# End units' transposes moved behind the next scores in two batches, low parts ahead of gathers, in a block-sparse attention kernel with a gated projection

## The chip, the cores and the metric

The kernel runs on one core of a Trainium2 chip. The metric is device time in microseconds (us) of one execution, the median over several runs. TensorE is PE in the profile (PEld is its weight load), VectorE is DVE, ScalarE is ACT, GpSimd is POOL, and SyncE, which issues most DMAs, is SP.

## The reference

Four batches, eight heads, 768 positions, head size 64. Attention is block sparse in blocks of 32: a block of queries sees its neighbours, the first and last block, and three drawn blocks. The first and last block of queries see everything. The result goes through a causal five-tap gate and two products with 512 x 512 weights.

```python
scores = scale * np.matmul(q, k.transpose(0, 1, 3, 2))
mask = np.abs(blk_i - blk_j) <= window
mask = mask | (blk_i == 0) | (blk_j == 0) | (blk_i == n_blocks - 1) | (blk_j == n_blocks - 1)
# and for every query block its three sampled key blocks
attn = np.exp(scores - max) / sum
x = np.matmul(attn, v)
gate_pre[s] = sum_k conv_w[k] * x[s - 4 + k]
out = (sigmoid(gate_pre) * (x @ w_val)) @ w_out
```

Everything is float32. The projections keep that precision by splitting each operand into a high part in a rounded format and a low part, and adding three products.

## The kernel before

The work is cut into 52 **units**, 13 a batch. Eleven units of a batch are pairs of inner query blocks. Two are **end units**, which hold the first and the last query block, see all 768 keys, and stand behind four to six pairs (`GLOB_AT`). Loop step n issues the scores of unit n, its softmax, the values of unit n-2, and the transposes of unit n-1, with pieces of the projection (`fill`, counted by the table `FILLS`) and of its preparation (`prepare`, counted by `STEPS`) between. A helper chains each engine's instructions in the order in which the Python code issues them, so each engine works through one list in order.

One unit: TensorE makes scores (tile `sc`, for an end unit four tiles `s`) in PSUM. VectorE takes the maxima (`mx`). ScalarE makes the exponentials (`pe`, for an end unit `first`, `rest`, `first`, `rest`). TensorE transposes them (`pt`, two buffers), ScalarE evicts them (`ptr`, three buffers), and TensorE multiplies with the values (`av`). VectorE divides (`rs`, `x`), TensorE transposes the result (`xp`), and ScalarE writes it to `xT`. An end unit has three groups of transposes and three evictions, a pair two. The PSUM tag `sc` has three buffers, which the scores and `xp` share.

The values of a pair's own and sampled blocks come in `vb` (three buffers) by two gathers, indirect DMAs that POOL issues (`load_values`). A gather for the unit three pairs on waits until `av` has read the buffer.

The projection of 384 rows (`project`, two a batch, eight in all, here called P1 to P8) has four groups `vp`, one for each of 128 channels f, and three row groups `op`. When group f is done, `evict(f)` makes `y` on VectorE (two buffers) and the high part `yh` on ScalarE. `second(f)` makes the low part `yl` on POOL. In the kernel before, `second(3)` is issued only after the first half of the first `op`, and the first `op` has the products with `yl` in its second half. `split` makes high and low parts `xh`, `xl` of the next rows in the same way; POOL has the `xl`. The gate's multiply-adds (`th`, 128 in all) are VectorE's. The two weight matrices arrive as words that VectorE decodes during batches 0 and 1 (`words`, with a cast on ScalarE).

`before_last_low` holds the gathers of a step back once only, in the step whose first half reaches the group behind the last `vp`. The functions `block_rows` and the branch on `SP_VALUES` are never entered, as the four tuples of `SP_VALUES` are empty; the tile `sv` is allocated all the same.

Of the kernel before, what the change touches and what calls it, by code (L numbers as in the profile page):

```python
# [19 lines left out]
NP = NB // 2  # L20
DM = H * D
DV = D + 1
CH = 4
# [20 lines left out]
SP_VALUES = ((), (), (), ())  # L44
REGS = 4
# [19 lines left out]
def attention_moe(ctx, tc, qb, kb, v, ve, sampled, w_val, conv_w, w_out, ident_in, slot_in, out):  # L65
# [33 lines left out]
    sb = const.tile([128, NB, NR, 2], I32, name="sb")  # L99
# [10 lines left out]
    ones = const.tile([128, 256], F32, name="ones")  # L110
# [9 lines left out]
    sf = const.tile([128, NR, NB], F32, name="sf")  # L120
# [11 lines left out]
    vm = const.tile([128, NR, NB], F32, name="vm")  # L132
    tmp = const.tile([128, NR, NB], F32, name="tmp")
# [19 lines left out]
    sv = const.tile([1, B, 2, NP - 1, NR], I32, name="sv")  # L153
    sk = tmp[0:1]

    def block_rows(b):

        dve.tensor_scalar_add(sk, sf[0:1], float((b - B) * NB))
        dve.tensor_tensor(out=sk, in0=sk, in1=vm[0:1], op=ALU.mult)
        for j in SP_VALUES[b]:  # L160
            dve.tensor_scalar_add(sv[:, b, j].rearrange("p i r -> p r i"), sk[:, :, 1 + j : NB - 1 : 2], float(B * NB))

# [10 lines left out]
    wv = [const.tile([128, CH, DM], F32R, name=f"wv{n}") for n in range(2)]  # L173
# [143 lines left out]
    def load_values(pr):  # L317
# [5 lines left out]
        if pr.p == 0 and SP_VALUES[b]:  # L323
            block_rows(b)
# [7 lines left out]
        for j, i in enumerate(PAIRS[pr.p]):  # L332
            if j in SP_VALUES[b]:
                near = i + (1 if j else -1)
                near = (b * NB + near if 0 < near < NB - 1 else B * NB) * BLK
                sp.dma_start(pr.vb[0:BLK, j, :], v[near : near + BLK, :])
                if pr.p % REGS == 0:
                    held[j] = nc.values_load_multi_w_load_instructions(
                        sv[0:1, b, j, pr.p : min(pr.p + REGS, NP - 1), :].rearrange("p i r -> p (i r)"), engines=[SP],
                        min_val=0, max_val=B * NB,  # L340
                        skip_runtime_bounds_check_because="block numbers are drawn from [0, 24)",
                    )[1]
                for r, reg in enumerate(held[j][pr.p % REGS * NR : pr.p % REGS * NR + NR]):
                    sp.dma_start(
                        pr.vb[BLK * (r + 1) : BLK * (r + 2), j, :],
                        v.rearrange("(n k) d -> n k d", k=BLK)[bass.ds(reg, 1)].rearrange("o k d -> (o k) d"),
                    )
                continue
            pool.indirect_dma_start(
                out=pr.vb[:, j, :], out_offset=None, in_=v,  # L350
                in_offset=bass.IndirectOffsetOnAxis(ap=idx[:, b, i : i + 1], axis=0),
            )
# [21 lines left out]
    def scores(un):  # L374
        pr = un.pr
        un.P = []
        if pr.glob:
# [10 lines left out]
            mx = three.tile([128, 2, 4], F32, tag="mx", name="mx")  # L388
            rest = five.tile([128, 2, 256], F32, tag="pr", name="rest")
            for h in range(2):  # L390
                dve.tensor_reduce(out=mx[:, h, 0:1], in_=lo[h], axis=AX.X, op=ALU.max, negate=True)
                dve.tensor_reduce(out=mx[:, h, 1:2], in_=hi[h][:, 0:256], axis=AX.X, op=ALU.max, negate=True)
                dve.tensor_tensor(out=mx[:, h, 2:3], in0=mx[:, h, 0:1], in1=mx[:, h, 1:2], op=ALU.min)
                first = five.tile([128, 512], F32, tag="pr", name="first")
                act.activation(rest[:, h, :], hi[h][:, 0:256], AF.Exp, bias=mx[:, h, 2:3])
                act.activation(first, lo[h], AF.Exp, bias=mx[:, h, 2:3])
                un.P.append(first)
            un.P.append(rest.rearrange("p h k -> p (h k)"))
            return
        sc = [ps_sc.tile([128, 2, 256], F32, tag="sc", name="sc") for _ in range(2)]  # L400
        kt = pr.kg.rearrange("p (t e) x -> p t e x", e=4)
        for a in range(2):
            for t in range(2) if a and pr.bt.b >= SPLIT else (slice(0, 2),):
                for g in range(4):
                    for h in range(2):
# [8 lines left out]
                        )  # L414
        mx = three.tile([128, 2, 4], F32, tag="mx", name="mx")
# [7 lines left out]
    def transposes(un):  # L423
        un.PT = []
        for p in un.P:
            pt = ps_pt.tile([128, 4, 128], F32, tag="pt", name="pt")
            for c in range(4):
                transpose(pt[:, c, :], p[:, 128 * c : 128 * c + 128], ident)
            t = three.tile([128, 4, 128], F32, tag="ptr", name="ptr")
            act.copy(t, pt)  # L430
            un.PT += [t[:, c, :] for c in range(4)]
            yield
# [118 lines left out]
    def project(m):  # L551
# [35 lines left out]
        evict(CH - 1)  # L587
        gating.discard(id(m))
# [14 lines left out]
        for r in range(m.n // 128):  # L603
# [3 lines left out]
            for f, yn, w in terms + [(CH - 1, yh, wo[0]), (CH - 1, yh, wo[1]), (CH - 1, yl, wo[0])]:  # L607
                matmul(op, yn[:, f, r * 128 : (r + 1) * 128], w[:, f, :], start=n == 0, stop=n == 11)
                n += 1
                if n == 6:  # L610
# [3 lines left out]
                    if r == 0:  # L614
                        second(CH - 1)
# [46 lines left out]
    def before_last_low(times):  # L662

        return may_project() and to_project[0][0].groups <= CH + 1 < to_project[0][0].groups + times
# [39 lines left out]
    for n in range(N + LAG_V):  # L704
# [25 lines left out]

        if n < N:
            scores(units[n])
        if n == 0:
# [12 lines left out]
        if n >= LAG_V and not before_last_low(int(FILLS[min(2 * n, len(FILLS) - 1)])):  # L746
            next_values()
        if 0 <= n - LAG_T < N:
            for half, _ in enumerate(transposes(units[n - LAG_T])):
# [3 lines left out]
                if n >= LAG_V:  # L753
# [68 lines left out]
```

## Time and profile before

| | us |
|---|---|
| median of three runs | 384.92 (383.56 to 385.92) |
| the profiled execution, time / span | 385.59 / 383.8 |
| busy: PE / PEld / DVE / ACT / POOL | 350.1 / 275.0 / 264.1 / 253.6 / 221.0 |

A row of the timeline has the start and the length of a run of like instructions, the engine, the operation with output and inputs, the count, and in brackets how long the engine stood idle before and what ended that. A row of the windows has the busy time of each engine in a stretch, with counts, then the granted TensorE clock (1.00 is 2.4 GHz), the DMA share and GB/s. TensorE's trace has two records for each matmul of the program. "issue" is time for which the profile shows no cause.

### The profile page before, as it was taken

How to read it: one execution, taken by the hardware profiler on the slowest of the kernel's cores; microseconds unless marked ns; L12 is line 12 of the kernel's file. 1: busy time of each engine (PE TensorE's matmuls, PEld its weight loads, DVE VectorE, ACT ScalarE, POOL GpSimd, SP SyncE). 2: the span in 40 equal slices, each digit the busy share in tenths (PEclk: the TensorE clock that was granted, in tenths of full speed). 3: DMA queues.
4: the chain of work that ended last, by engine and by line, in shares of the span. 5: the costliest groups of instructions: out<-in, count | busy, mean ns of one | idle time of the engine just before them, and what ended most of it. 6: DMA issues, size and time to landing. Idle time of an engine off the chain costs nothing.

```text
span 383.8 us, 15523 instructions
## 1 busy us (share of the span) xinstructions
PE 350.1 (91%) x6274; PEld 275.0 (72%) x6274; DVE 264.1 (69%) x546; ACT 253.6 (66%) x619; POOL 221.0 (58%) x309
## 2 busy tenths in 40 slices
PE   8788869878967999999899979999999999999895
PEld 7365556556646887788679857787787879789794
DVE  4346476866897779477978877656769877959520
ACT  1857697887788758765776756756666766565321
POOL 1885566897486486757553266556633753444640
PEclk9969999999999999999999989999999999999999
DMA  7997982999991546789786337788773373110102
GB/s 235 300 300 238 344 278 59 280 263 300 320 297 52 133 126 195 217 286 286 205 241 213 81 108 226 203 271 246 205 203 112 96 224 113 33 56 30 56 28 84
DMA packets 52584, 72.37 MB, mean 189 GB/s; under 512 B 6944, under 2 KB 34720, under 8 KB 52512
## 3 DMA queue, kind: packets, MB, share of 16 engines
q1 hardware_dynamic: 44896, 47.69, 40.7%
q0 software_dynamic: 7040, 23.43, 21.1%
q8 instruction: 50, 0.82, 0.9%
q10 hardware_dynamic: 576, 0.24, 0.2%
q14 instruction: 22, 0.18, 0.2%
HBM read 65.05 MB, written 6.29 MB: 186 GB/s over the span
## 4 chain that ended last, share of the span: by engine, by line
PE 65%; DVE 16%; ACT 7%; issue 6%; POOL 3%; DMA 1%; ACTq 1%; DVEq 0%
PE av L83 13%; PE op L83 13%; PE vp L83 13%; PE sc L83 11%; PE pt L83 9%; DVE th L83 7%; DVE mx L83 4%; PE xp L83 3%; PE s L83 3%; ACT pe L83 2%; ACT ptr L83 1%; DVE x L83 1%; POOL vb L83 1%; DMA sb<-in_sampled 1%; ACT kg L83 1%
## 5 line engine op out<-in xcount | busy, mean ns | idle before, releaser
L83 POOL DMA_INDIRECT vb<-in_v,idx x88 | 89.7, 1019 | 91.4 <-PE av L83 66.1
L83 DVE SCALAR_TENSOR_TENSOR th<-xT,cw,th 128x384 f32<-128x384 f32 x128 | 111.0, 875 | 11.8 <-ACT th L83 9.5
L83 ACT ACTIVATE pe<-sc,mx 128x256 f32<-128x256 f32 x176 | 69.0, 476 | 47.0 <-DVE mx L83 42.2
L83 DVE TENSOR_REDUCE mx<-sc 128x2 f32<-128x512 f32 x88 | 56.5, 683 | 47.9 <-PE sc L83 36.7
L83 ACT COPY ptr<-pt 128x512 f32<-128x512 f32 x112 | 64.9, 602 | 4.5 <-PE pt L83 4.0
L83 POOL TENSOR_TENSOR yl<-y,yh 128x384 fp32r<-128x384 f32 x32 | 34.7, 1091 | 38.6 <-ACT yh L83 38.2
L83 POOL COPY kg<-k 128x256 f32<-128x256 f32 (+1 forms) x143 | 52.2, 402 | 8.1 <-DMA k<-in_k 8.0
L83 PE MATMUL op<-wo,yh 128*128 128x512 f32 x192 | 53.7, 401 | 0.3 <-DVE y L83 0.3
L83 PE MATMUL sc<-kg,qc 64*32 64x256 f32 x1408 | 52.0, 392 | 2.1 <-issue 1.0
L83 PE MATMUL pt<-ident,pe 128*128 128x128 f32 x352 | 52.1, 283 | 0.4 <-issue 0.4
L83 PE MATMUL vp<-xh,wv 128*128 128x384 f32 x256 | 51.3, 341 | 0.0
L83 PEld LDWEIGHTS av<-va,ptr 128*32 128x32 f32 (+1 forms) x1056 | 31.7, 120 | 24.5 <-issue 14.9
L83 PE MATMUL av<-va,ptr 128*32 128x65 f32 (+1 forms) x1056 | 41.3, 229 | 4.5 <-ACT ptr L83 2.2
L83 PEld LDWEIGHTS pt<-ident,pe 128*128 128x128 f32 x352 | 39.6, 142 | 7.0 <-issue 0.9
L83 PEld LDWEIGHTS vp<-xh,wv 128*128 128x128 f32 x256 | 44.1, 188 | 0.2
L83 PE MATMUL av<-vb,ptr 128*32 128x65 f32 x1408 | 40.0, 225 | 2.6 <-issue 2.4
L83 PEld LDWEIGHTS op<-wo,yh 128*128 128x128 f32 x192 | 34.6, 188 | 7.5 <-DVE y L83 0.8
L83 POOL TENSOR_TENSOR xl<-xT,xh 128x384 fp32r<-128x384 f32 x32 | 35.4, 1111 | 6.1 <-ACT xh L83 5.9
L83 PEld LDWEIGHTS sc<-kg,qc 64*32 64x32 f32 x1408 | 23.3, 108 | 17.6 <-issue 9.8
L83 PE MATMUL op<-wo,yl 128*128 128x512 f32 x96 | 32.0, 413 | 3.3 <-POOL yl L83 3.3
L83 PEld LDWEIGHTS av<-vb,ptr 128*32 128x32 f32 x1408 | 31.1, 112 | 4.8 <-issue 3.2
L83 DVE SCALAR_TENSOR_TENSOR y<-th,vp 128x384 f32<-128x384 f32 x32 | 17.5, 548 | 23.2 <-PE vp L83 12.8
(72 smaller groups left out, 448.8 us busy)
## 6 DMA issues: line engine op xcount, KB each, us to landing
kg<-in_k SPq DMA_DIRECT2D x165, 64.0 KB
vn<-in_v SPq DMA_DIRECT2D x12, 520.0 KB
qc<-in_q SPq DMA_DIRECT2D x48, 128.0 KB
k<-in_k SPq DMA_DIRECT2D x12, 512.0 KB
out<-ot SPq DMA_DIRECT2D x23, 256.0 KB
va<-in_v SPq DMA_DIRECT2D x44, 130.0 KB
wst<-in_w_val SPq DMA_DIRECT2D x4, 512.0 KB
wst<-in_w_out SPq DMA_DIRECT2D x4, 512.0 KB
```

What stands on the lines that cost most here:

```text
L83: made = getattr(self.eng, name)(*args, **kwargs)
```

## The change

In batches 0 and 1 (`HI_MOE` is 2) the transposes of an end unit are issued right behind the scores of the next unit, ahead of that unit's softmax and of the values of the unit before. Two of the three evictions stand on ScalarE ahead of the next unit's exponentials and the third behind them. Since `softmax` is now a function of its own, nothing else moves by that split. `ptr` has five buffers in place of three. `second(3)` follows `evict(3)` at once, and all gathers of a step in which the low parts of a projection are completed stand behind the half in which that happens. To pay for the two buffers, small tiles of the start live in buffers that are used later (`y`, `wv`), and the dead code goes. The tables are unchanged.

```diff
-    ones = const.tile([128, 256], F32, name="ones")
+    wv = [const.tile([128, CH, DM], F32R, name=f"wv{n}") for n in range(2)]
+    ones = wv[0][:, 0, 0:256].bitcast(F32)
...
-            t = three.tile([128, 4, 128], F32, tag="ptr", name="ptr")
+            t = five.tile([128, 4, 128], F32, tag="ptr", name="ptr")
...
         evict(CH - 1)
+        second(CH - 1)
...
-                    if r == 0:
-                        second(CH - 1)
...
-    def before_last_low(times):
-
-        return may_project() and to_project[0][0].groups <= CH + 1 < to_project[0][0].groups + times
+    def last_lows(fills):
+
+        if may_project():
+            groups = to_project[0][0].groups
+            for half, times in enumerate(fills):
+                if groups <= CH < groups + times:
+                    return half
+                groups += times
+        return -1
...
+        early = None
         if n < N:
             scores(units[n])
+            if n and units[n - 1].pr.glob and units[n - 1].pr.bt.b < HI_MOE:
+                early = transposes(units[n - 1])
+                next(early)
+                next(early)
+            softmax(units[n])
+            if early:
+                next(early)
...
-        if n >= LAG_V and not before_last_low(int(FILLS[min(2 * n, len(FILLS) - 1)])):
+        lows = last_lows([int(FILLS[i]) for i in (2 * n, 2 * n + 1) if i < len(FILLS)])
+        if n >= LAG_V and lows < 0:
             next_values()
         if 0 <= n - LAG_T < N:
-            for half, _ in enumerate(transposes(units[n - LAG_T])):
+            for half, _ in enumerate(range(3) if early else transposes(units[n - LAG_T])):
...
-                if n >= LAG_V:
+                if n >= LAG_V and min(half, 1) >= lows:
                     next_values()
```

TensorE at the end units of batch 0, from the values of a pair (`va`, `vb`) to the scores behind the second end unit's transposes (`vn` are the end unit's values). Before:

```order
L83 MATMUL av<-va_149,ptr 64x65 x8
L83 MATMUL av<-vb,ptr 32x65 x16
L83 MATMUL pt<-ident,first 128x128 x8
L83 MATMUL pt<-ident,rest 128x128 x4
L83 MATMUL xp<-ident,x 128x128 x2
L83 MATMUL sc<-kg_145,qc 32x256 x16
L83 MATMUL av<-vn,ptr 32x65 x48
L83 MATMUL pt<-ident,first 128x128 x8
L83 MATMUL pt<-ident,rest 128x128 x4
L83 MATMUL sc<-kg_146,qc 32x256 x16
```

And with the change:

```order
L81 MATMUL pt<-ident,first 128x128 x8
L81 MATMUL pt<-ident,rest 128x128 x4
L81 MATMUL av<-va_147,ptr 64x65 x8
L81 MATMUL av<-vb,ptr 32x65 x16
L81 MATMUL xp<-ident,x 128x128 x2
L81 MATMUL sc<-kg_143,qc 32x256 x16
L81 MATMUL pt<-ident,first 128x128 x8
L81 MATMUL pt<-ident,rest 128x128 x4
L81 MATMUL av<-vn,ptr 32x65 x48
L81 MATMUL sc<-kg_144,qc 32x256 x16
```

Both groups of twelve transposes passed one group of `av`.

ScalarE in the next step, from the first end unit's evictions to the exponentials of the pair behind the end units. Before:

```order
L83 COPY ptr<-pt 128x512 x3
L83 CAST wv_150<-words 128x512
L83 COPY xT<-xp 128x4x64
L83 ACTIVATE qc<-qc 128x256
L83 ACTIVATE pe<-sc,mx 128x256 x4
```

And with the change (the first end unit's evictions stand further up):

```order
L81 CAST wv_86<-words 128x512
L81 COPY xT<-xp 128x4x64
L81 ACTIVATE qc<-qc 128x256
L81 COPY ptr<-pt 128x512 x2
L81 ACTIVATE pe<-sc,mx 128x256 x4
L81 COPY ptr<-pt 128x512
```

Two evictions of the second end unit came ahead of the exponentials, behind the cast of the weights.

POOL in P2 (second projection of batch 0; P4 and P1 are alike). Before:

```order
L83 DMA vb<-in_v,idx 128x520 x2
L83 TENSOR_TENSOR yl<-y,yh 128x384
L83 DMA vb<-in_v,idx 128x520 x2
L83 TENSOR_TENSOR yl<-y,yh 128x384 x2
L83 TENSOR_TENSOR xl<-xT,xh 128x384
L83 TENSOR_TENSOR yl<-y,yh 128x384
L83 TENSOR_TENSOR xl<-xT,xh 128x384
L83 DMA vb<-in_v,idx 128x520 x2
L83 TENSOR_TENSOR xl<-xT,xh 128x384
```

And with the change:

```order
L81 DMA vb<-in_v,idx 128x520 x2
L81 TENSOR_TENSOR yl<-y,yh 128x384 x4
L81 TENSOR_TENSOR xl<-xT,xh 128x384
L81 DMA vb<-in_v,idx 128x520 x4
L81 TENSOR_TENSOR xl<-xT,xh 128x384 x2
```

Two gathers went from between the low parts to behind the first `xl`, and one `xl` behind all four gathers. In P3 two gathers that stood ahead of the third low part now stand behind the fourth and one `xl`. In P5 to P8 only the fourth `yl` and an `xl` change places.

## Rows read from the trace of the kernel before

**Rows 1.** The page: the chain that ended last, by engine.

```profile
PE 65%; DVE 16%; ACT 7%; issue 6%; POOL 3%; DMA 1%; ACTq 1%; DVEq 0%
```

**Rows 2.** The windows: the stretch behind the end units of batch 1.

```profile
124.00:164.00 40.00, 40.00 (x638) 32.60 (x637) 28.89 (x61) 29.72 (x76) 27.24 (x39) 1.00 0.62 168
```

**Rows 3.** The timeline at the end units of batch 0.

```profile
45.70 1.07 PE L83 MATMUL s<-k,qc 64*32 64x256 f32 x25 [0.76 <-issue]
...
47.91 1.09 PE L83 MATMUL pt<-ident,first 128*128 128x128 f32 x8
...
49.45 0.42 DVE L83 TENSOR_SCALAR words<-wst 128x512 f32<-128x512 f32 x1
...
50.97 0.69 DVE L83 SCALAR_TENSOR_TENSOR words<-words,wst 128x512 int32<-128x512 int32 x1
...
51.07 0.66 PE L83 MATMUL pt<-ident,rest 128*128 128x128 f32 x4 [2.06 <-ACT kg L83]
...
52.30 0.62 ACT L83 CAST wv<-words 128x512 fp32r<-128x512 f32 x1
...
52.90 1.57 PE L83 MATMUL av<-vn,ptr 128*32 128x65 f32 x96
...
53.85 1.57 ACT L83 ACTIVATE pe<-sc,mx 128x256 f32<-128x256 f32 x4 [0.34 <-DVE mx L83]
...
56.54 0.66 PE L83 MATMUL pt<-ident,rest 128*128 128x128 f32 x4 [1.05 <-ACT ptr L83]
...
58.91 0.62 PE L83 MATMUL sc<-kg,qc 64*32 64x256 f32 x4 [0.70 <-issue]
```

**Rows 4.** The timeline at the end units of batch 1, and three groups over the whole span: the last of the three VectorE operations that follow `av` and the evictions (busy us, mean ns), and between them the gate's multiply-adds by tile (ns, shortest/median/longest).

```profile
109.67 1.09 PE L83 MATMUL pt<-ident,first 128*128 128x128 f32 x8
...
112.34 4.77 DVE L83 SCALAR_TENSOR_TENSOR th<-xT,cw,th 128x384 f32<-128x384 f32 x3
...
113.55 0.66 PE L83 MATMUL pt<-ident,rest 128*128 128x128 f32 x4 [2.79 <-ACT ptr L83]
...
120.04 0.66 PE L83 MATMUL pt<-ident,rest 128*128 128x128 f32 x4 [2.07 <-ACT ptr L83]
...
L83 DVE TENSOR_TENSOR x<-av,rs 128x256 f32<-128x256 f32 x48 | 20.4, 424 | 1.7
...
L83 DVE SCALAR_TENSOR_TENSOR th<-xT,cw,th x128: 605/619/4453, 86.9 to 358.8; 128x384 f32<-128x384 f32 x128
...
L83 ACT COPY ptr<-pt 128x512 f32<-128x512 f32 x112 | 64.9, 602 | 4.5 <-PE pt L83 4.0
```

**Rows 5.** The timeline in P2.

```profile
174.66 0.96 POOL L83 DMA_INDIRECT vb<-in_v,idx  x1 [1.87 <-PE av L83]
...
176.89 1.99 POOL L83 TENSOR_TENSOR yl<-y,yh 128x384 fp32r<-128x384 f32 x2
...
177.94 0.56 DVE L83 SCALAR_TENSOR_TENSOR y<-th,vp 128x384 f32<-128x384 f32 x1 [2.11 <-POOL yl L83]
178.41 3.77 DVE L83 SCALAR_TENSOR_TENSOR th<-xT,cw,th 128x384 f32<-128x384 f32 x1
...
180.76 1.00 POOL L83 TENSOR_TENSOR xl<-xT,xh 128x384 fp32r<-128x384 f32 x1
...
182.10 1.27 DVE L83 TENSOR_REDUCE mx<-sc 128x2 f32<-128x512 f32 x2
...
187.89 0.67 PE L83 MATMUL s<-k,qc 64*32 64x256 f32 x16 [1.69 <-ACT xT L83]
```

**Rows 6.** The timeline in P3 (first projection of batch 1).

```profile
215.69 0.51 ACT L83 CAST yh<-y 128x384 fp32r<-128x384 f32 x1 [1.02 <-DVE y L83]
...
219.66 0.55 ACT L83 CAST yh<-y 128x384 fp32r<-128x384 f32 x1
...
220.90 1.00 POOL L83 TENSOR_TENSOR yl<-y,yh 128x384 fp32r<-128x384 f32 x1
...
221.95 0.50 PE L83 MATMUL op<-wo,yl 128*128 128x512 f32 x1 [1.06 <-POOL yl L83]
...
223.85 0.50 PE L83 MATMUL op<-wo,yl 128*128 128x512 f32 x1 [0.94 <-POOL yl L83]
```

**Rows 7.** The windows: a wait of TensorE and the stretch behind it, in P3 and at the end units of batch 1.

```profile
221.00:224.60 3.60, 1.71 (x6) 0.89 (x6) 3.60 (x1) 0.52 (x2) 3.60 (x4) 0.96 0.60 185
224.60:228.50 3.90, 3.90 (x100) 2.58 (x100) 2.46 (x5) 2.32 (x7) 1.25 (x3) 0.60 0.13 39
...
109.60:113.50 3.90, 1.16 (x20) 0.85 (x8) 3.76 (x10) 2.78 (x7) 3.42 (x7) 1.00 0.91 279
113.50:118.00 4.50, 4.42 (x142) 3.39 (x142) 4.43 (x5) 3.05 (x8) 4.03 (x7) 1.00 0.47 155
```

**Rows 8.** The timeline in P7, the last projection but one, behind all units.

```profile
354.13 0.51 ACT L83 CAST yh<-y 128x384 fp32r<-128x384 f32 x1 [0.30 <-DVE y L83]
...
355.77 1.31 POOL L83 TENSOR_TENSOR yl<-y,yh 128x384 fp32r<-128x384 f32 x1
...
357.13 0.50 PE L83 MATMUL op<-wo,yl 128*128 128x512 f32 x1 [1.34 <-POOL yl L83]
```

**Rows 9.** The timeline at the start: the first gather, and the first multiplication that reads what it fetched.

```profile
12.15 1.13 POOL L83 DMA_INDIRECT vb<-in_v,idx  x1 [0.19 <-issue]
...
20.15 0.67 PE L83 MATMUL av<-vb,ptr 128*32 128x65 f32 x9
```

More of the change, by code (lines that the diff above doesn't have):

```diff
@@ L42 @@
 COPIED = [{0: POOL, 1: POOL, 2: POOL, 3: ACT, 4: ACT, 5: ACT}, {0: POOL, 1: POOL, 2: ACT}, {}, {}]
-SP_VALUES = ((), (), (), ())
-REGS = 4
 FILLS = (
@@ L96, in attention_moe @@
     matmul, transpose = pe.matmul, pe.transpose
-    sb = const.tile([128, NB, NR, 2], I32, name="sb")
+    spare = two.tile([128, TS], F32, tag="y", name="spare")
+    vm, tmp, sf = (
+        spare[:, NB * NR * n : NB * NR * (n + 1)].rearrange("p (r i) -> p r i", r=NR) for n in range(3)
+    )
+    sb = two.tile([128, TS], F32, tag="y", name="sb").bitcast(I32)[:, 0 : NB * NR * 2]
+    sb = sb.rearrange("p (i r w) -> p i r w", i=NB, r=NR)
     src = sampled.bitcast(I32)
@@ L119, in attention_moe @@
     dve.tensor_copy(sm, sb[0:1, :, :, 0].rearrange("p i r -> p (i r)"))
-    sf = const.tile([128, NR, NB], F32, name="sf")
     dve.tensor_copy(sf, sb[:, :, :, 0].rearrange("p i r -> p r i"))
@@ L131, in attention_moe @@
     dve.memset(valid[0:32, NB - 2 : NB - 1], 0.0)
-    vm = const.tile([128, NR, NB], F32, name="vm")
-    tmp = const.tile([128, NR, NB], F32, name="tmp")
     dve.tensor_scalar(out=vm, in0=sf, scalar1=0.0, scalar2=None, op0=ALU.not_equal)
@@ L152, in attention_moe @@
     idx = const.tile([128, B, NB], I32, name="idx")
[L153 to L161, printed above, removed]
     def indices(b):
@@ L172, in attention_moe @@
     va = [const.tile([128, H * DV], F32, name=f"va{n}") for n in range(VRING)]
-    wv = [const.tile([128, CH, DM], F32R, name=f"wv{n}") for n in range(2)]
     wo = [const.tile([128, CH, DM], F32R, name=f"wo{n}") for n in range(2)]
@@ L322, in load_values @@
             indices(b)
-        if pr.p == 0 and SP_VALUES[b]:
-            block_rows(b)
         vt = va[pr.seq % VRING]
@@ L332, in load_values @@
         for j, i in enumerate(PAIRS[pr.p]):
[L333 to L348, printed above, removed]
             pool.indirect_dma_start(
@@ L375, in scores @@
         pr = un.pr
-        un.P = []
         if pr.glob:
@@ L387, in scores @@
                     )
[L388 to L398, printed above, removed]
+            un.scores = lo, hi
             return
-        sc = [ps_sc.tile([128, 2, 256], F32, tag="sc", name="sc") for _ in range(2)]
+        sc = un.scores = [ps_sc.tile([128, 2, 256], F32, tag="sc", name="sc") for _ in range(2)]
         kt = pr.kg.rearrange("p (t e) x -> p t e x", e=4)
@@ L414, in scores, with softmax @@
                         )
+    def softmax(un):
+        un.P = []
+        if un.pr.glob:
+            lo, hi = un.scores
+            mx = three.tile([128, 2, 4], F32, tag="mx", name="mx")
+            rest = five.tile([128, 2, 256], F32, tag="pr", name="rest")
+            for h in range(2):
+                dve.tensor_reduce(out=mx[:, h, 0:1], in_=lo[h], axis=AX.X, op=ALU.max, negate=True)
+                dve.tensor_reduce(out=mx[:, h, 1:2], in_=hi[h][:, 0:256], axis=AX.X, op=ALU.max, negate=True)
+                dve.tensor_tensor(out=mx[:, h, 2:3], in0=mx[:, h, 0:1], in1=mx[:, h, 1:2], op=ALU.min)
+                first = five.tile([128, 512], F32, tag="pr", name="first")
+                act.activation(rest[:, h, :], hi[h][:, 0:256], AF.Exp, bias=mx[:, h, 2:3])
+                act.activation(first, lo[h], AF.Exp, bias=mx[:, h, 2:3])
+                un.P.append(first)
+            un.P.append(rest.rearrange("p h k -> p (h k)"))
+            return
+        sc = un.scores
         mx = three.tile([128, 2, 4], F32, tag="mx", name="mx")
```

## The prediction

> **What bounds the kernel now.** I read the chain of waits first. The reader is to see that TensorE carries 65% of it and no DMA queue more than 1% [rows 1], so that an edit counts where TensorE waits for somebody. Then I read the windows. Behind the end units of batch 1 TensorE is busy 40.00 of 40.00 us [rows 2]: time saved ahead of that should come out at the end, and later only single waits are left to win. The timelines of the places that the diff touches give those waits: four before the third transposes of an end unit, 2.06 and 1.05 us in batch 0, 2.79 and 2.07 us in batch 1 [rows 3, 4]; one before scores in P2, 1.69 us [rows 5]; two before low-part products in P3, 1.06 and 0.94 us [rows 6]; one in P7, 1.34 us [rows 8].
>
> **End units, batch 0.** The third transposes need a PSUM buffer that ScalarE's first eviction frees. That eviction stood behind four exponentials and copies of keys. Now it stands ahead of them, and both groups of transposes move ahead of `av`. `av` takes 47.91 - 46.77 = 1.1 us, from the end of the end unit's scores (45.70 + 1.07) to the transposes [rows 3]. So the 2.06 us go, but `av` now ends about 1.9 us later: 1.09 + 0.66 for the transposes [rows 3] and 0.1 for the first eviction. What follows `av` on VectorE is late next: `x`, with 0.42 us of its own [rows 4] and two shorter operations, 1.0 together (at most three times 0.42), and behind it the decoding of a weight, which runs from 49.45 to 50.97 + 0.69 = 51.66 now [rows 3]. It would start at about 46.8 + 1.9 + 1.1 + 1.0 = 50.8, 1.4 later, and end at 53.0, so the cast that waits for it comes at 53.0 in place of 52.30. From the cast to the exponentials ScalarE takes 53.85 - 52.30 = 1.55 us [rows 3]; the new order puts two evictions more between, 0.55 to 0.6 each [rows 4]. So the exponentials start at about 55.6 in place of 53.85. TensorE waits for the first of those evictions until 55.1, then does the third transposes (0.66) and 96 records of `av` (1.57) [rows 3], and reaches the next scores at 57.3. Now it reaches them at 56.54 + 0.66 = 57.2 [rows 3]. Gain: -0.1. Those scores now stop for 0.70 us for no cause that is shown [rows 3]. If that pause does not come back, the gain is up to 1.0; if only the late exponentials count, it is -1.7. I take -0.2, as nothing in the change touches that pause.
>
> **End units, batch 1.** Here VectorE is late: three multiply-adds take 4.77 us, to 117.1, and the maxima wait behind them. One of them alone takes 0.62 (the median) [rows 4], so 2.9 us are lost, and the timeline of POOL has three `xl` beside them. With the change the transposes start 1.1 us earlier, the third group at about 110.1 in place of 113.55, `av` ends at about 112.0 and `x` at 112.9. The multiply-adds start at 112.9 in place of 112.34 [rows 4]. But the two gathers wait for the same `av` and stand ahead of two of the three `xl`, which so move from about 113 to 114.4, and the multiply-adds get through before, at about 114.8. The maxima follow at once, 2.3 us earlier. ScalarE does casts until about 116.0, then two evictions; the exponentials are done by 118.7. TensorE does the second end unit's third transposes at 116.6 in place of 120.04 [rows 4], then `av` (1.57 [rows 3]) before the next scores, which start at 118.9 where they now start at 120.7. Gain 1.8; I take 1.7. The bounds are 0 (VectorE not freed) and the two waits, 2.79 + 2.07 = 4.9 [rows 4].
>
> **P2.** VectorE's `y` waited 2.11 us for a low part that stood behind two gathers [rows 5]. The multiply-add behind it then took 3.77 us, to 182.18, and VectorE came to the maxima at 182.10. Three POOL subtractions ran back to back over it, the last from 180.76 to 181.76 [rows 5]. The scores of an end unit, which wait for the `xT` that ScalarE does behind all this, lost 1.69 us. With the change the second low part follows the first at once, about 4 us earlier than 176.89 (it holds an earlier multiply-add and its maxima up by 1.0, for which TensorE does not wait). `y` comes as soon as its product is done, at 177.2. The third low part holds the multiply-add until about 179.0, when POOL waits for the fourth `yh`. So the maxima start when their scores are there, 180.1, 2.0 us earlier, and 1.4 of the 1.69 go (bounds 0 and 1.69). The Trainium skill, "SBUF — State Buffer", "Who interferes with whom", says that a VectorE operation with two SBUF inputs and a GpSimd one exclude each other for one whole instruction, whichever came first. By that alone the multiply-add would have waited for one subtraction of 1.0 us, the order on POOL would not decide, and the sum would be 1.4 lower; the row shows three subtractions in a train.
>
> **P3.** The third low part had its input at 216.2 (215.69 + 0.51) and started at 220.90, behind gathers. The fourth has its input at 220.2 (219.66 + 0.55). With the change they run at 216.3 and at 220.3 to 221.3, at worst 221.7 if a multiply-add holds them. TensorE wants them at 220.9 and 221.9, so both waits go: 2.0 us [rows 6] (at least 1.0). Behind these waits the granted clock was 0.60 over 3.90 us, most of it at the lower level of 1.2 GHz, and TensorE had been busy 1.71 of the 3.60 us ahead of it [rows 7]. At full clock the work of that stretch takes 3.90 x 0.60 = 2.3 us, so 1.6 more are to be had; I take 1.4, since some of its records do not follow the clock. P3: 3.4 (at least 1.0, at most 3.6).
>
> **P7.** The fourth low part has its input at 354.13 + 0.51 = 354.6, but starts at 355.77, behind an `xl` [rows 8]. With the change it runs first, 1.31 us long, to 355.95. TensorE waits 0.2 in place of 1.34: 1.1 (0.9 to 1.34).
>
> **At no cost.** P1, P4, P5 and P6 have no wait of TensorE at the places moved (P1: 40.00 of 40.00 [rows 2]), and an `xl` that comes later serves a product over 10 us away. The later gathers have 7 to 15 us left until `av` reads them, three steps on; at the start one was issued and read within 20.15 - 12.15 = 8.0 us [rows 9]. SP's list is the same, and its waits move with what frees the buffers. Two more `ptr` buffers cost nothing, since the tiles that made room are read before their buffers' next use.
>
> **The sum.** -0.2 + 1.7 + 1.4 + 3.4 + 1.1 = 7.4. From the profiled execution, 385.59 - 7.4 = 378.2. That execution stands 0.67 above the median, so **377.5** on the median's footing. All low bounds give -1.7 + 0 + 0 + 1.0 + 0.9 = 0.2, all high ones 1.0 + 4.9 + 1.7 + 3.6 + 1.3 = 12.5, or 384.7 and 372.4.
>
> **The rivals.** (1) The end units give nothing: the wait before the third transposes is replaced by waits for `x` and for evictions. 384.92 - 5.9 + 0.2 to 2 = 379.2 to 381. For it: the longer path through the decoding in batch 0. Against: VectorE's 4.77 us in batch 1, which a later `xl` should end [rows 4].
> (2) VectorE is not freed: POOL's four low parts and `xl` make an even longer train, so batch 1 and P2 give nothing, and P3 gives its two waits without the clock. 2.0 + 1.1 - 0.2 = 2.9, so 382.0. For it: the 3.77 us [rows 5]. Against: each low part waits for its own `yh`, which leaves gaps.
> (3) The clock falls in the new order, behind an end unit's transposes, where TensorE still waits in short pieces. One such fall costs what P3's cost, 1.4, two 2.9: 379 to 380.4. Against: 1.16 busy of 3.90 us was followed by 1.00 [rows 7]. The Trainium skill, "TensorE: Matmul & The Clock Gate", "Part 1: The HAM clock gate", has the half clock as the state of an idle engine that activity ends; the trace agrees in P3 and not at the end units.
> (4) Slower: the gathers come too late. In P1, P2 and P4 they move back by 6 to 9 us, P2's from 174.66 [rows 5] to about 181. If one lands more than about 10 us after issue, `av` waits: at 14 us, 4 us at each of three places, 12 - 7.4 = 4.6 slower, 389.5. Against: 8.0 us at the start [rows 9].
> (5) The saved time is lost again before the end, to a load or a pause of the unshown kind: 384.9.
>
> **How the numbers follow.** Chances: forecast 0.45, (1) 0.17, (2) 0.15, (3) 0.08, (4) 0.08, (5) 0.07. About 1%, 3.85 us, is what can be told from no change. The forecast, (1) and (3) end below 381.1: 0.70, of which 0.01 each goes to the other sides for their edges: faster 0.68. Same: (2), (5) and the edge, 0.23. Slower: (4) and the edge, 0.09. The range leaves out (4) and (5) and the far high bounds: 375.0 to 383.0.
>
> **What would show it.** Right: in the profile after, no wait for a low part in P3, granted clock 1.00 behind it, no multiply-add of 3.77 us in P2 and less than 0.5 us before its scores, P7's wait near 0.2, and the third transposes of batch 1 with waits near 1 us. Wrong: `av` of pairs waiting for a gather, the clock at 0.60 in batch 1, or the waits at the end units found again before `xp`.

## The result, and the profile after

The change made the kernel slightly slower: 388.08 us, the median of 21 runs, against 385.89 of 21 runs of the kernel before on the same chip, a ratio of 1.0067 (95% interval 1.0046 to 1.0089). The forecast was 377.5, 7.4 less than before. Ratios with their intervals leave out runs more than 1.5% above the fastest of their kernel, and medians are of all runs, so the two can differ a little. Two later sets gave the same kernel a ratio of 0.989; the experiments are about that.

The page after, its span, busy times and the chain by engine (rows 1 of before):

```profile
span 386.6 us, 15513 instructions
...
PE 350.4 (91%) x6274; PEld 274.5 (71%) x6274; DVE 257.5 (67%) x546; ACT 253.4 (66%) x619; POOL 220.6 (57%) x309
...
PE 66%; DVE 13%; DMA 7%; ACT 6%; issue 5%; SPq 2%; POOL 1%; ACTq 1%; POOLq 0%; DVEq 0%
```

VectorE is busy 6.6 us less, and POOL has 1% of the chain where it had 3%: the low parts of P2 and P7 have left it, two of P3 are in it still. DMA has 7% in place of 1%; these are loads in the first 110 us, where the change lost 0.50 us (first row of the table below). Much of what was aimed at did happen. The timeline in P7 and at the end units of batch 1 (against [rows 8, 4]):

```profile
357.79 0.51 ACT L81 CAST yh<-y 128x384 fp32r<-128x384 f32 x1 [0.31 <-DVE y L81]
358.38 1.09 POOL L81 TENSOR_TENSOR yl<-y,yh 128x384 fp32r<-128x384 f32 x1 [0.20 <-ACT yh L81]
...
110.58 0.66 PE L81 MATMUL pt<-ident,rest 128*128 128x128 f32 x4 [0.82 <-ACT ptr L81]
113.26 1.92 DVE L81 SCALAR_TENSOR_TENSOR th<-xT,cw,th 128x384 f32<-128x384 f32 x3
115.35 2.92 POOL L81 TENSOR_TENSOR xl<-xT,xh 128x384 fp32r<-128x384 f32 x3
116.58 0.66 PE L81 MATMUL pt<-ident,rest 128*128 128x128 f32 x4 [0.69 <-ACT ptr L81]
116.99 1.60 DVE L81 TENSOR_SCALAR words<-wst 128x512 f32<-128x512 f32 x1
118.66 1.09 PE L81 MATMUL sc<-kg,qc 64*32 64x256 f32 x32
120.81 1.28 DVE L81 TENSOR_REDUCE mx<-sc 128x2 f32<-128x512 f32 x2
121.80 0.88 PE L81 MATMUL av<-vn,ptr 128*32 128x65 f32 x48 [1.34 <-issue]
122.77 1.09 PE L81 MATMUL pt<-ident,pe 128*128 128x128 f32 x8
```

The last three of these places before:

```profile
118.23 0.41 DVE L83 TENSOR_SCALAR words<-wst 128x512 f32<-128x512 f32 x1
120.62 1.09 PE L83 MATMUL sc<-kg,qc 64*32 64x256 f32 x32
123.15 1.09 PE L83 MATMUL pt<-ident,pe 128*128 128x128 f32 x8
```

In P7 the low part follows its high part at once. In batch 1 the two waits of 2.79 and 2.07 us are 0.82 and 0.69, the three multiply-adds take 1.92 us in place of 4.77, and the next scores start at 118.66 where they started at 120.62. Two microseconds are won there, and lost again within one unit: the maxima of these scores stand behind the decoding of a weight and start at 120.81, and the pair's transposes come at 122.77, against 123.15 before. The decoding was slowed as well: its first operation took 1.60 us in place of 0.41, beside POOL's three `xl`, so the train that no longer holds the multiply-adds holds the decoding. TensorE's `av` of the end unit also stops for 1.34 us, for no cause that is shown. All eight traces of kernels with early transposes in batch 1 have that stop at the same place (1.14 to 2.62 us), and none without them has it.

What was lost lies in P1 to P4. In P2, VectorE, ScalarE and POOL waited until 184.6 to 184.8 for TensorE, whose transposes had run from 181.83 to 182.49 and from 183.71 on (timeline after, P2):

```profile
181.72 0.96 POOL L81 DMA_INDIRECT vb<-in_v,idx  x1
181.83 0.66 PE L81 MATMUL pt<-ident,pe 128*128 128x128 f32 x4
182.99 0.95 POOL L81 DMA_INDIRECT vb<-in_v,idx  x1 [0.30 <-issue]
184.60 0.16 DVE L81 TENSOR_SCALAR rs<-av 128x4 f32<-128x4 f32 x1 [2.39 <-PE pt L81]
184.66 0.59 ACT L81 COPY ptr<-pt 128x512 f32<-128x512 f32 x1 [1.44 <-PE pt L81]
184.83 0.95 POOL L81 DMA_INDIRECT vb<-in_v,idx  x1 [0.90 <-PE pt L81]
185.35 5.07 DVE L81 SCALAR_TENSOR_TENSOR th<-xT,cw,th 128x384 f32<-128x384 f32 x4
187.05 1.95 POOL L81 TENSOR_TENSOR xl<-xT,xh 128x384 fp32r<-128x384 f32 x2
190.61 1.01 DVE L81 TENSOR_REDUCE mx<-s 128x1 f32<-128x512 f32 x2
194.31 0.65 PE L81 MATMUL pt<-ident,pe 128*128 128x128 f32 x4 [2.30 <-ACT rest L81]
```

The end unit's maxima before:

```profile
187.53 0.68 DVE L83 TENSOR_REDUCE mx<-s 128x1 f32<-128x512 f32 x1
```

VectorE so began its four multiply-adds late, ran into POOL's two `xl`, and came to the end unit's maxima 3.1 us later than before (190.61 against 187.53). TensorE waited 2.30 us for `rest`, and the windows show the granted clock at 0.67 behind that:

```profile
190.40:194.30 3.90, 1.61 (x8) 1.00 (x6) 3.76 (x11) 1.57 (x4) 3.58 (x5) 1.00 0.98 302
194.30:199.50 5.20, 5.19 (x60) 3.28 (x61) 2.96 (x7) 2.78 (x6) 0.00 (x0) 0.67 0.72 240
```

In P1, P3 and P4 `av` came in pieces beside moved gathers, with idle time that no row explains. P1 and P3 after:

```profile
147.21 1.10 POOL L81 DMA_INDIRECT vb<-in_v,idx  x1 [0.16 <-issue]
148.37 0.56 PE L81 MATMUL av<-va,ptr 128*64 128x65 f32 x11
148.62 0.95 POOL L81 DMA_INDIRECT vb<-in_v,idx  x1 [0.30 <-issue]
149.26 0.28 PE L81 MATMUL av<-va,ptr 128*64 128x65 f32 x2 [0.32 <-issue]
150.13 1.29 DVE L81 TENSOR_REDUCE mx<-sc 128x2 f32<-128x512 f32 x2 [1.71 <-remote]
...
227.41 0.99 POOL L81 DMA_INDIRECT vb<-in_v,idx  x1
228.71 0.95 POOL L81 DMA_INDIRECT vb<-in_v,idx  x1 [0.30 <-issue]
228.72 0.31 PE L81 MATMUL av<-va,ptr 128*32 128x65 f32 x3 [0.45 <-issue]
230.25 1.29 DVE L81 TENSOR_REDUCE mx<-sc 128x2 f32<-128x512 f32 x2 [2.83 <-remote]
```

VectorE waited in the same moments: its maxima needed scores whose matmuls had ended at 148.44 and 227.76. The trace also records the semaphore updates, the signals by which engines and queues release one another. In 12 to 345 us it has some 140 stretches of more than 0.45 us without any recorded update after, and 137 before; they are called **pauses** below. While a gather is being issued there are 9 to 10 updates per us, outside 21. Both kernels of this set have the pauses.

A pause is one of the record. The engines' instructions of that stretch make 1568 updates after, of which 1280 are recorded; in `tiles_only`, a run below without the pauses, 1574 of 1590 are. The work that waits for the others went on, so updates are missing from the record, and it does not show that no signal passed. Nor can the releasers in brackets be relied on there. What the starts of the instructions do show is that engines stood still beside gathers; the pauses mark the sets in which that happened.

A table by stage sums this up. It subtracts the start of the same TensorE instruction in two traces, so that a row is what a stage lost (+) or gained (-), in us. The first two columns are against the trace of before: the change, and the best version found in the end, in a run that also had the pauses. The other three, without pauses, are against a run with the order of before (`tiles_only`): the change twice, and the best version. Each column is one trace. From P1 on, the two of the change agree within 0.3 us; with pauses no version was traced twice.

| stage | after | third_ot3_2 | again | again_2 | third_ot3 |
|---|---|---|---|---|---|
| start, to the second end unit's scores of batch 1 | +0.50 | +1.32 | +1.71 | +1.31 | -0.28 |
| to P1's first `vp` | -0.86 | +0.07 | -0.61 | +0.07 | +0.37 |
| P1, to P2's first `vp` | +1.07 | +0.57 | -0.02 | +0.03 | -0.01 |
| P2, to P3's first `vp` | +3.62 | -1.32 | -1.11 | -1.12 | -1.38 |
| P3, to its second `op` | -1.45 | -1.41 | -3.68 | -3.71 | -3.70 |
| to P4's first `vp` | +0.02 | +0.05 | +1.57 | +1.56 | +1.55 |
| P4, to P5's first `vp` | +0.71 | -0.28 | -0.41 | -0.43 | -0.01 |
| P5 and P6, to P7's first `vp` | +0.05 | +0.03 | +0.26 | -0.01 | -0.07 |
| P7, to P8's first `vp` | -1.24 | -1.23 | -1.28 | -1.27 | -1.26 |
| to the end | +0.32 | +0.02 | +0.35 | +0.29 | -0.02 |

From P1's first `vp` to the end the kernel before took 256.1 us with pauses, and its order (`tiles_only`) 254.9 without; the change took 259.2 with and 250.2 to 250.5 without. So where the pauses are, the kernel before took 1.2 us longer and the change some 9.

### The profile page after: what moved, and what is told of

The parts are those of the page before. It is cut to its first block, busy times and chain, and to the rows that moved or that the text cites. A ratio compares the mean times of both kernels' runs of the same rounds, so it can differ in the third digit from the quotient of the medians.

```text
span 386.6 us, 15513 instructions
## 1 busy us (share of the span) xinstructions
PE 350.4 (91%) x6274; PEld 274.5 (71%) x6274; DVE 257.5 (67%) x546; ACT 253.4 (66%) x619; POOL 220.6 (57%) x309
## 4 chain that ended last, share of the span: by engine, by line
PE 66%; DVE 13%; DMA 7%; ACT 6%; issue 5%; SPq 2%; POOL 1%; ACTq 1%; POOLq 0%; DVEq 0%
PE op L81 16%; PE vp L81 14%; PE av L81 13%; PE pt L81 10%; PE sc L81 9%; DVE th L81 5%; DVE mx L81 5%; DMA k<-in_k 4%; PE xp L81 2%; ACT ptr L81 2%; PE s L81 2%; DMA kg<-in_k 2%; SPq L81 1%; ACT pe L81 1%; DMA wst<-in_w_out 1%
## 5 line engine op out<-in xcount | busy, mean ns | idle before, releaser
L81 DVE SCALAR_TENSOR_TENSOR th<-xT,cw,th 128x384 f32<-128x384 f32 x128 | 103.2, 815 | 11.8 <-ACT th L81 9.5
L81 PE MATMUL op<-wo,yh 128*128 128x512 f32 x192 | 54.7, 408 | 0.2
L81 PE MATMUL sc<-kg,qc 64*32 64x256 f32 x1408 | 50.8, 387 | 3.1 <-POOL kg L81 2.1
L81 PE MATMUL av<-va,ptr 128*32 128x65 f32 (+1 forms) x1056 | 42.6, 226 | 8.0 <-issue 3.8
L81 ACT CAST yh<-y 128x384 fp32r<-128x384 f32 x32 | 16.9, 527 | 21.3 <-DVE y L81 21.3
```

The source lines that it names most:

```text
L81: made = getattr(self.eng, name)(*args, **kwargs)
```

## The experiments

Theory 1 is that the moved gathers cause the losses in P1 to P4, theory 2 that the early transposes do. Each set has its own runs of the kernel before, so ratios are compared.

**First set**, kernel before 380.59 us. The four edits, as differences from the changed kernel: (a) `early_lowpart`, gathers back; (b) `low_gather`, no early transposes; (c) `early_only`, gathers and fourth low part back; (d) `tiles_only`, all of it back but the buffers and tiles.

```diff
(a), (c), (d)
-        if n >= LAG_V and lows < 0:
+        if n >= LAG_V and not before_last_low(int(FILLS[min(2 * n, len(FILLS) - 1)])):
...
-                if n >= LAG_V and min(half, 1) >= lows:
+                if n >= LAG_V:
(b), (d)
-            if n and units[n - 1].pr.glob and units[n - 1].pr.bt.b < HI_MOE:
+            if n and units[n - 1].pr.glob and units[n - 1].pr.bt.b < 0:
(c), (d)
-        second(CH - 1)
...
+                    if r == 0:
+                        second(CH - 1)
```

> The changed kernel with its gathers back where they stood before (the early transposes, the fourth low part right behind its eviction and the five buffers stay). Theory 1: what the change loses in the first four projections comes from the moved gathers alone: stalls of TensorE in av beside a gather in P1 (1.3 us), P3 (1.7) and P4 (1.1), and in P2 two low parts of the next rows pushed behind the gathers, over VectorE's multiply-adds (2.5 us of wait and 1.6 of clock). By it these 8 us go and part of P3's 3.2 us goes back (the third low part is behind gathers again): 388.1 - 8.1 + 1 to 3.2 = 381.0 to 383.2 where the kernel before has 385.9, a ratio of 0.987 to 0.993, no stall of av in P1 and P4, and no wait of 2.3 us for rest in P2. Theory 2: the losses come from the early transposes, which shift the steps behind them against the transfers, or are chance: then the losses stay and P3's gain goes, 388 to 391, a ratio of 1.006 to 1.013.

> The changed kernel without the early transposes (the fourth low part and the late gathers stay). Theory 1 (the late gathers cause the losses): the losses of 8 us in P1 to P4 stay, the gains in P2 (0.4), P3 (3.2) and P7 (1.3) stay, and the 1.2 us of the end units go: 385.9 + 8.1 - 4.9 = 389.1, a ratio of 1.008, with stalls of av beside gathers in P1, P3 and P4. Theory 2 (the early transposes cause them): 385.9 - 4.9 = 381.0, a ratio of 0.987, without these stalls.

> The early transposes alone, with the five buffers and the moved tiles; low parts and gathers as before. Both theories take the gain at the end units from the trace of the change: 0.45 us in batch 0 and 0.9 in batch 1. Theory 1: nothing else changes, 385.9 - 1.3 = 384.6, a ratio of 0.997. Theory 2: the losses in P1 to P4 are found here too: 385.9 - 1.3 + up to 8 = 388 to 392, a ratio of 1.006 to 1.016.

> Only the five buffers and the small tiles that moved to make room; all work in the order of before. Theory 1: nothing, a ratio of 1.000 (0.998 to 1.002). The trace of the change is 0.87 us late already at 40 us, ahead of the first moved transpose; if the moved tiles of the start cause that, the ratio is 1.002 and the delay is found again at 40 us; if it is chance, it is not.

Measured: `early_lowpart` 0.9966 (0.9918 to 1.0015), `low_gather` 0.9894 (0.9850 to 0.9938), `early_only` 0.9988 (0.9930 to 1.0045), `tiles_only` 1.0001 (0.9955 to 1.0047). By its ratio `low_gather` speaks for theory 2, `early_only` against it: neither part loses when it is alone. The traces said what both theories had missed: none of the four has the pauses (30 to 44 in place of some 140), and `low_gather`, with the late gathers, has no stall of `av` in P1 or P4. And `early_lowpart` lost 5.9 us in P5, at a place of its own (below). The buffers and tiles cost nothing; the 0.87 us at 40 us were chance, since this start differs by several us between any two traces.

**Second set**, kernel before 379.19 us: the change again, without early transposes again, early transposes in batch 1 only (`== 1` for `< HI_MOE`), and the fourth low part alone ((a) and (b) together).

> The changed kernel once more, beside the version without the early transposes, which was 1.06% faster than the kernel before in another set of runs, while the change as a whole was 0.67% slower in its own. Theory A (the early transposes undo the gain of the other parts): again slower than the kernel before or equal to it, a ratio of 1.000 to 1.009, and 1 to 2% above the version without them. Theory B (the sets differ: in the first one all engines' semaphore updates paused by about 0.6 us at a time beside gathers, in the traces of before and of the change alike, and the change put gathers beside av; the second set shows few such pauses): where the kernel before comes out near 380.6 us the change is 0.5 to 1.3% faster, 375.6 to 378.7, and where it comes out near 386 the ratio is again near 1.007.

> The version without the early transposes a second time, for a comparison with the change in the same set. Theory A: a ratio of 0.989 again, whatever the kernel before takes. Theory B: 0.989 where the kernel before is near 380.6 us, near 1.008 where it is near 386.

> The changed kernel with the early transposes in batch 1 only. The trace of the change gives 0.9 us to those of batch 1 and 0.45 to those of batch 0. If these gains are real, the time lies between the change and the version without them, 0.45 us above the change. Theory A: with one of two batches undone, half of the loss of the early transposes stays, a ratio of 0.995 to 1.000. Theory B: a ratio within 0.2% of the change's.

> The fourth low part right behind its eviction, with the five buffers; no early transposes, gathers where they were. P7 gives its wait (1.3 us measured in the trace of the change), P3 the second of its two waits (0.94) and nothing of the clock, as the third low part is still behind the gathers: 2.2 us, a ratio of 0.994. If the gathers' move is worth the rest of P3's 3.2 us and 2 us in P2, as the trace of the version with both shows, this version is 0.4 to 0.8% slower than that one.

Measured: `again` 0.9887 (0.9840 to 0.9934), `low_gather_2` 0.9885 (0.9829 to 0.9940), `early_b1` 0.9917 (0.9877 to 0.9957), `low_only` 0.9941 (0.9885 to 0.9998). Theory A, that the early transposes undo the gain, falls. The same program is 1.1% faster here and was 0.7% slower there. Its P1 and P2 in this trace:

```profile
142.25 0.97 POOL L81 DMA_INDIRECT vb<-in_v,idx  x1 [0.16 <-issue]
143.24 0.69 PE L81 MATMUL av<-va,ptr 128*64 128x65 f32 x16
143.52 0.94 POOL L81 DMA_INDIRECT vb<-in_v,idx  x1 [0.30 <-issue]
143.86 0.67 PE L81 MATMUL av<-vb,ptr 128*32 128x65 f32 x32
...
176.41 2.57 DVE L81 SCALAR_TENSOR_TENSOR th<-xT,cw,th 128x384 f32<-128x384 f32 x4
184.22 0.66 PE L81 MATMUL pt<-ident,pe 128*128 128x128 f32 x4 [0.23 <-ACT rest L81]
```

The gathers stand beside `av` in P1 as in the trace after (the first 1.0 us ahead of it in place of 1.16, the second 0.28 behind its start in place of 0.25), and `av` runs through. In P2 VectorE is not kept waiting, its four multiply-adds are through in 2.57 us, 1.4 us before POOL's two `xl` (180.41), and TensorE waits 0.23 us where it waited 2.30.

**P5.** In `early_lowpart`, ScalarE's eviction of P4's last row group waited for a store, and the first `vp` of P5 for that eviction; SyncE had issued the store behind six loads of keys:

```profile
263.37 2.96 SPq L81 DMA_DIRECT2D kg<-in_k  x6
266.43 0.38 SPq L81 DMA_DIRECT2D out<-ot  x1
...
271.00 0.60 ACT L81 ACTIVATE ot<-op 128x512 f32<-128x512 f32 x1 [5.62 <-DMA out<-ot]
...
271.65 2.35 PE L81 MATMUL vp<-xh,wv 128*128 128x384 f32 x8 [4.13 <-ACT ot L81]
```

One try issues the stores ahead of the step's loads of keys (**third set**, kernel before 381.49 us), with the low part alone, with the whole change, and with the gathers moved in P3 only:

```diff
+        store()
         if n == 0:
             more_keys()
...
         until("scaled", n + (SCALE_AHEAD if n else 1), scale)
-        store()
...
(third_*)
+        third = bool(to_project) and to_project[0][0].third
-        lows = last_lows([int(FILLS[i]) for i in (2 * n, 2 * n + 1) if i < len(FILLS)])
+        lows = last_lows([int(FILLS[i]) for i in (2 * n, 2 * n + 1) if i < len(FILLS)]) if third else -1
...
```

> Only the fourth low part moved (as in the run of that part alone), and SyncE issues a projection's stores ahead of the step's loads of keys. In two traces with the fourth low part moved and the gathers where they were, ScalarE's eviction of the last row group of P4 waited 4 to 6 us for a store to land, which SyncE had issued behind six loads of keys, P5's first vp stopped for it, and the clock fell: 5.9 and 6.8 us lost between P5's first and third group. Theory S (SyncE's list is what is late): the store is issued about 3 us earlier, P5 loses nothing, a ratio of 0.994 - 0.016 = 0.978 (0.975 to 0.985). Rival (the transfer itself is slow there, or the keys are late instead): P5 still waits, or a scores' wait for keys takes its place, a ratio of 0.990 to 0.998.

> The whole change with the stores ahead of the loads of keys. In the change's own traces the store of P4 is issued 3 us ahead of P5 and P5 loses 0 to 0.3 us, so both theories expect little here: a ratio of 0.988 (0.984 to 0.992). If the kernel before comes out near 386 us with pauses of all engines' semaphore updates beside gathers, 1.004 to 1.009 is expected for this version, as for the change.

> Early transposes, the fourth low part behind its eviction, stores ahead of keys, and the gathers moved in P3 alone. P2's 1.9 us were found without moved gathers too, and P1 and P4 had nothing to win, so by the forecast's terms the time equals the whole change's where pauses are rare: 0.988 (0.984 to 0.992). Where they are frequent (the kernel before near 386), the trains of four gathers in P1, P2 and P4 are gone with what they cost (1.3, 4.1 and 1.1 us): 0.985 to 0.993 instead of 1.007.

> The same without the early transposes. If these are worth the 1.5 us that were forecast for them, 0.992; if they are worth nothing, as two pairs of runs say (0.4 us apart, and alone 0.1%), 0.988, the same as with them within 0.3%.

Measured: 0.9984 (0.9930 to 1.0038), 0.9964 (0.9920 to 1.0008), 1.0008 (0.9959 to 1.0056) and 0.9962 (0.9906 to 1.0018). The two that have a twin without the edit are no better than it (0.9941 and 0.9887). P5 loses nothing any more (0.0 us in all four), but other stages do: 1.1 to 1.8 us of the gain in P2 are gone, and P4 takes 2.0 to 6.6 us more than in `tiles_only`. In P4 VectorE waits for a load of queries (`qc`) 5.8 to 6.6 us, and TensorE for the `y` behind it, 1.7 to 3.5 us; in `third_store` the granted clock is 0.56 for 3.8 us after that. SyncE issues the queries from the same list. In `third_store`:

```profile
243.41 1.36 DVE L81 TENSOR_SCALAR qc<-qc 128x256 f32<-128x256 f32 x1 [6.57 <-DMA qc<-in_q]
```

A wait was moved, not removed.

The other try gives the tile a third buffer and leaves SyncE's list alone (**fourth set**, kernel before 379.35 us), beside the change a third time:

```diff
-            ot = two.tile([128, DM], F32, tag="ot", name="ot")
+            ot = three.tile([128, DM], F32, tag="ot", name="ot")
...
-            t = five.tile([128, 4, 128], F32, tag="ptr", name="ptr")
+            t = three.tile([128, 4, 128], F32, tag="ptr", name="ptr")
```

> The whole change a third time. Theory B (pauses of the semaphore updates beside gathers decide the sign): if the kernel before comes out below 382 us, a ratio of 0.985 to 0.994, av without stalls beside gathers in P1, P3 and P4; if it comes out near 386 with pauses, 1.003 to 1.009. The rival, that the two sets differ by something that has nothing to do with gathers, predicts either ratio in either state.

> The fourth low part behind its eviction and the late gathers, no early transposes, three ptr buffers as before, and a third buffer for the tile that holds a row group on its way out (ot). If P5's loss (1.6 to 1.8 us in this version) is ScalarE's wait for a store that has not landed, the third buffer ends it without touching SyncE's list: 0.988 less 0.004 = 0.984 (0.980 to 0.988). If the loss is SyncE's list itself, which is late with keys too, the time comes back as another wait: 0.988. In the state with pauses: 1.003.

> The same with the gathers where they were. P5 lost 5.9 and 6.8 us here, with the clock. If the store is the cause: 0.994 less 0.016 = 0.978 (0.975 to 0.985), the fastest of all, and the late gathers are then worth little. If another wait takes its place, 0.990 to 0.995. In the state with pauses, where the late gathers are thought to do the harm, 0.985 to 0.992, and so over 1% below the version with late gathers.

Measured: `again_2` 0.9886 (0.9846 to 0.9926), `low_gather_ot3` 0.9872 (0.9808 to 0.9936), `low_only_ot3` 0.9892 (0.9848 to 0.9936). In `low_only_ot3` ScalarE evicts without a wait and P5 follows:

```profile
266.65 0.62 ACT L81 ACTIVATE ot<-op 128x512 f32<-128x512 f32 x1
...
268.74 1.56 PE L81 MATMUL vp<-xh,wv 128*128 128x384 f32 x8
```

So P5's loss is the wait for a landed store. What it costs on the mean is open: the ratio moved by 0.005, not by the 0.016 expected, while the medians of all runs went from 379.11 to 373.90 us beside kernels before of 379.19 and 379.35, about 0.014.

**The best version**: the fourth low part behind its eviction, gathers moved in P3 alone, three buffers for `ot` and for `ptr`, no early transposes. It ran in two sets, beside the kernel before at 379.53 and at 385.69 us.

> The parts that paid, together: the fourth low part behind its eviction, the gathers moved in P3 alone, three buffers for ot, three for ptr, no early transposes. By the traces it keeps P2's 1.9 us, P3's 3.7 and P7's 1.3, loses nothing in P5, and does not give back the 1.5 us that VectorE and POOL take at the end of P3 in the whole change: 1.3 to 1.5 us better than the whole change, a ratio of 0.985 (0.981 to 0.988) where the kernel before is near 380 us. If the savings are lost again further on, 0.988 to 0.990. In the state with pauses beside gathers (the kernel before near 386), where only P3's gathers could do harm: 0.985 to 0.993.

> The best version once more. A ratio of 0.980 to 0.987 where the kernel before is near 380 us. If it is near 386 with pauses of the semaphore updates beside gathers: 0.985 to 0.993 if the trains of gathers in P1, P2 and P4 did the harm in the first set, 1.000 or above if something else did.

Measured: 373.19 us, 0.9802 (0.9755 to 0.9850), and 382.12 us, 0.9945 (0.9911 to 0.9979). The first ratio says more than its trace explains: from P1 on its stages are worth 4.9 us (1.3%), where those of `low_only_ot3`, without any moved gather, are worth 5.3. The rest may be the start, or chance, as this version has six runs in that set. The 1.5 us behind P3's second `op` were lost in it too, against what was expected. The second set has the pauses again: the trace shows some 140, 9 updates per us beside gathers, and the kernel before takes what it took in the set of the result. With pauses the version still gains, at the upper edge of what was expected. `av` in P1 there:

```profile
149.77 0.95 POOL L81 DMA_INDIRECT vb<-in_v,idx  x1 [0.30 <-issue]
150.10 0.60 PE L81 MATMUL av<-va,ptr 128*64 128x65 f32 x10
151.11 0.44 PE L81 MATMUL av<-va,ptr 128*64 128x65 f32 x6 [0.42 <-issue]
```

The first two columns of the table speak for theory 1, where there are pauses. With P2's gathers where they were, P2 gains 1.32 us where the whole change lost 3.62: 4.9 us apart. P4 is 1.0 us apart in the same sense, P1 0.5. Together that is 6.4 of the 6.7 us that separate the two from P1 on (+3.1 and -3.6). In P3 both have the late gathers, and both keep 1.4 us of the 3.7 that runs without pauses show. This is not proof: the two versions also differ in the early transposes and in the buffers, each stands for one trace, and late gathers everywhere without the early transposes did not come to run with pauses. What makes the pauses was not found.

## Why the prediction was wrong

**P7** (1.1 forecast) was right, 1.24 to 1.28 us in every trace. **P3** (3.4) was right at its place where there are no pauses: 3.7, the clock included. But the fourth low part alone gives 2.46 of that (`low_only_ot3`), and in the whole change 1.6 us were lost again ahead of P4. In the run of the result the clock came back too, but the next `av`, beside the late gathers, took 3.31 us (227.70 to 231.01) where it takes 1.09 in `again`, and 1.45 us are left. **P2** (1.4) was right without pauses: 1.92 us at its scores, of which 1.1 to 1.4 reach P3. It came with the fourth low part alone (-1.39 in `low_only_ot3`), so the early fourth low part did it and not the later gathers, to which the forecast owed it: the number was right by luck.

**The step that failed is "At no cost"**, and in it the sentence on the later gathers. It priced a gather by when its data land. No `av` waited for a landing: in the trace after, the last packet of each gather ended at least 6.9 us ahead of the `av` that reads it, from P1 on. So rival (4) had the sign and the places (P1, P2, P4) with the wrong mechanism. What the trace shows in its place is loss while POOL issues: in this set engines stood still beside moved gathers, in the middle of `av` and ahead of a hand-over, and in the sets without pauses they did not. Lost in P1 1.1 us, in P2 3.6 in place of a gain (its wait for `rest` and the clock), in P3 2.2 of the 3.7, in P4 0.7. That the moved gathers did this rests on their places and on the two columns of the table; why engines stand still beside a gather in some sets stays open. The missing updates leave room for the recording itself to be the cause, and no run tells.

The trace of before had shown it, had I asked. Ahead of P4 its `av` stops beside a gather, as it does at 73, 84 and 88 us, and I had passed over them as idle time without a cause:

```profile
242.84 0.98 POOL L83 DMA_INDIRECT vb<-in_v,idx  x1 [0.30 <-issue]
...
243.46 0.29 PE L83 MATMUL av<-vb,ptr 128*32 128x65 f32 x3 [0.26 <-issue]
```

**End units** (1.5 together). The waits ahead of the third transposes went as forecast, and the gain did not last. By the ratios rival (1) is the likelier here: with and without the early transposes they are 0.9887 and 0.9885 in one set, and alone they give 0.9988 beside 1.0001. But each has an interval of about 0.5%, 1.9 us, to either side, so 1.5 us cannot be ruled out by them. The sum stopped at the next scores, one step short of what takes over: the decoding ahead of the maxima, slowed by POOL's train, and the stop in `av`.

**P5** was also in "At no cost", as "SP's list is the same, and its waits move with what frees the buffers". They do not move as far: when TensorE gains 4 us SyncE's stores stay behind, and a version can lose 6 us there. In the whole change it lost 0.0 to 0.3.

The Trainium skill, "SBUF — State Buffer", "Who interferes with whom", gives the ports that VectorE and POOL share to whoever issues first, for the whole instruction. The trace does not agree: in P2 after, four multiply-adds took 5.07 us, 2.5 more than the 2.57 without a train beside them, and POOL's two `xl` ran back to back for 1.95. One of the four, begun at 186.71 and so 0.34 us ahead of the first `xl`, took 3.05 us. VectorE did not get its turn between the two: the train decides, as the row of before said [rows 5].

The range, 375.0 to 383.0, does not hold 388.08. The forecast of a gain does hold where there are no pauses: 374.3 and 375.0 us against 379.2 and 379.4, 4.3 to 4.9 us of the 7.4. The end units' 1.5 and the 1.6 that P3 lost again are about the rest.

## What to carry to other kernels

Price a moved transfer by its issue as well as by its landing: look at what the other engines do beside each issue in the trace, and take idle time without a cause as a sign to be explained before work is moved towards it. Follow a gain past the next wait to the first engine that is still late, and let a store have a spare buffer before the compute engine is made faster. Count the signals that a record holds against those that the program makes before its gaps are read as waits. Time a change of one per cent in more than one set of runs; here its sign turned from set to set.

## What the runs showed of the hardware that was not expected

In two sets the kernel before took 385.7 and 385.9 us, in the five others, on four chips, 379.2 to 381.5. The traces of the first kind have some 140 stretches of more than 0.45 us without any recorded semaphore update (median 0.6 us), those of the other 30 to 44; while a gather is issued they have 9 to 10 recorded updates per us against 24 to 26. They hold some 18% fewer of the engines' own updates than their instructions make, the others 1%. A gather's issue takes the same 0.97 us in both. In P2 after, VectorE and ScalarE went on up to 2.2 us behind the end of TensorE's transposes. From P1 on, the pauses come with only 1.2 us more for the kernel before; the rest of its 5 us lies ahead of P1, where traces without pauses differ by 5 us among themselves too.

VectorE's one-input operation on `qc` was held by POOL's train as well, 2.93 us in place of 0.3 to 0.5, in the whole change between P3 and P4 (timeline of `again`):

```profile
222.25 2.93 DVE L81 TENSOR_SCALAR qc<-qc 128x256 f32<-128x256 f32 x1
222.71 1.98 POOL L81 TENSOR_TENSOR xl<-xT,xh 128x384 fp32r<-128x384 f32 x2
227.26 0.41 PE L81 MATMUL xp<-ident,x 128*128 128x128 f32 x2 [0.98 <-DVE x L81]
```
